# Weight conversion's low word moved to GpSimd, and a planner that changes its durations after the first batch

## The chip, the cores and the metric

The kernel runs on one core of one Trainium2 chip. The metric is the device time of one execution in microseconds (us); the median of several executions counts. TensorE is called PE, VectorE DVE, ScalarE ACT, GpSimd POOL, and SyncE, which issues most of the transfers here, SP.

## What is computed

```python
scores = scale * q @ k.T                       # 4 batches, 8 heads, 576 tokens, 64 wide
bias = -(cum[:, :, :, None] - cum[:, :, None, :])   # cum: running sum of max(s, 0)
scores = where(causal, -1e9, scores + minimum(bias, 0))
attn = softmax(scores) @ v                     # x: 2304 tokens x 512
h = x @ w_in                                   # 512 -> 2048
x = (h * (1 / (1 + exp(-1.702 * h)))) @ w_out  # 2048 -> 512
P = 8 rounds of row and column scaling of exp(x @ w_gate - max)   # 2304 x 8
out = sum over e of P[:, e] * (maximum(x @ w1[e], 0) @ w2[e])      # 8 experts
```

`w_in` and `w_out` come as 64-bit floats, all other inputs as 32-bit floats.

## The kernel before

The program has three stretches. In the first, attention is computed and its result goes through the first feed-forward layer (`w_in`, `w_out`), interleaved on PE. In the second, the last two token blocks go through that layer as one wide block. In the third, the eight experts run over three blocks of 768 tokens each; this is the longest one, and its products are built from seven half-size products each.

Attention goes batch by batch, and in a batch first over the first 256 query rows of the 8 heads, then over the other 320, so that there are 64 heads-and-halves, called heads in the code (`heads`, line 570 and on). A head has one or three units. A unit's scores are two matmuls into a PSUM bank (`sp<-one`, `sp<-two`; in the first eight heads one matmul `sp<-kf`); DVE adds the mask and takes the minimum (`sm<-sp,mask`), ACT takes the exponential (`ACTIVATE sm`), PE transposes (`turn`, tile `tp`), ACT and DVE split the result into two half-precision parts (`ph`, `pl`; in the first 14 heads a plain copy `pf`), and PE multiplies with the values (`op`). In the third unit of a later head, POOL clears 64 columns of `sm` before the transposes (`MEMSET sm`). A head's queries and keys are loaded (`kq`), rounded by ACT or DVE (`one`), their remainder taken by DVE, and one half copied by a transfer (`two<-one`).

The feed-forward layer takes 256 tokens and 256 hidden columns at a time: `mm1` (24 matmuls in two halves into `hp`), a tanh on ACT, a product on DVE, a split into `gh` and `gl`, and `mm2` (24 matmuls into `acc`). Its weights must first be converted. There are 32 chunks of 128 x 512 numbers (`conv`, line 525). A chunk is loaded as pairs of 32-bit words into `st`; ACT rebases the exponent of the high words (`Prelu`), ACT turns the top byte of each low word into three bits (`Copy` with a scale and an offset, line 536), DVE joins the two (`t<-st`), and `split` makes the rounded part (`wih`, `woh`, by ACT or DVE) and the remainder (`wil`, `wol`, by DVE).

The order on every engine is made by a planner at build time (`Sequencer`). Each call is recorded with a duration from `cost` and the calls that it depends on; `issue` keeps a clock for each engine; `settled` says when a tile will be ready, and adds 200 ns. The main loop (line 2033 and on) asks at the planner's present PE time which of six things can go next, in a fixed order: scale of the values, transposes of finished tokens, values, turn, scores, and only then a piece of the feed-forward layer. So that layer's matmuls fill PE where the planner believes attention isn't ready. Work of the other engines is held with a rank and issued as its engine comes free; conversion and the early preparation of the experts' weights have rank 2, the last. Until the layer's first piece, PE gets filler matmuls (`unread<-mask`) where its recent use is under half. `any_copy` gives a copy to DVE or ACT, whichever has less queued in the planner's clocks. From `begin_second` on (line 1888) `seq.fine` is set and other durations hold.

## Time and profile before

| | |
|---|---|
| median of 3 executions | 2006.13 us (2004.4 to 2006.52) |
| the profiled execution | 2004.02 us, of which the span from first to last instruction is 2002.3 us |
| busy in the span | PE 98%, weight loads 79%, DVE 74%, ACT 62%, POOL 4% |
| mean granted PE clock | 0.994 of full speed |
| HBM traffic | 157 GB/s over the span |

The profiled execution is the fastest of those shown; it lies 2.1 us under the median. A matmul's busy time overlaps that of its neighbours, so a busy PE is a PE that has work, not one at its peak. Times within the span count from its first instruction.

### The profile page before, as it was taken

What the parts mean: (1) busy time and instruction counts of PE and PEld (TensorE: products, weight loads), DVE (VectorE), ACT (ScalarE), POOL (GpSimd) and SP (SyncE); (2) the same over time, 40 slices, a digit from 0 to 9 for tenths busy, and PEclk for the clock granted to TensorE, in tenths of its full rate; (3) what the DMA queues carried; (4) which work ended last, traced back from release to release, by engine and by line L of the source; (5) the groups of instructions that cost most, each with busy time, mean ns of one, the idle gap of its engine ahead of it and who ended that gap; (6) DMA issues with size and microseconds to landing.
All of it is one profiled execution on the core that took longest, in us unless ns stands there. A gap on an engine that the chain in (4) does not pass through costs nothing.

```text
span 2002.3 us, 41146 instructions
## 1 busy us (share of the span) xinstructions
PE 1964.1 (98%) x15805; PEld 1578.6 (79%) x15805; DVE 1471.9 (74%) x3421; ACT 1249.3 (62%) x2576; POOL 87.2 (4%) x144
## 2 busy tenths in 40 slices
PE   7989999999999999999999999999999999999999
PEld 6888999999998677777777777777777777777777
DVE  7787888887853676988877766776786876777656
ACT  6787667675634575666666666656666666665333
POOL 1000000000000000000000111111101001111000
PEclk9999999999999999999999999999999999999999
DMA  8455455444226454475475566667557556566331
GB/s 253 126 187 176 123 141 155 130 130 118 76 69 213 156 198 151 159 257 182 156 256 145 131 184 176 181 171 203 161 130 244 152 156 181 163 172 182 119 129 43
DMA packets 230100, 322.12 MB, mean 161 GB/s; under 512 B 38272, under 2 KB 156224, under 8 KB 229904
## 3 DMA queue, kind: packets, MB, share of 16 engines
q1 hardware_dynamic: 216944, 295.90, 45.1%
q0 software_dynamic: 12960, 23.60, 8.2%
q8 instruction: 124, 2.03, 0.4%
q14 instruction: 72, 0.59, 0.1%
HBM read 230.85 MB, written 84.34 MB: 157 GB/s over the span
## 4 chain that ended last, share of the span: by engine, by line
PE 73%; DVE 10%; ACT 6%; DMA 2%; issue 1%; SPq 0%; ACTq 0%; DVEq 0%
PE C L307 16%; PE A L307 16%; PE D L307 16%; PE B L307 8%; PE hp L307 6%; PE acc L307 3%; ACT h L307 2%; PE accw L307 2%; DVE h L307 2%; PE op L307 1%; PE sp L307 1%; PE tp L307 1%; DVE hst L307 1%; DVE sa L307 1%; DMA kq<-in_qk_dram 1%
## 5 line engine op out<-in xcount | busy, mean ns | idle before, releaser
L307 PEld LDWEIGHTS <-h 128*128 128x128 f16 x6048 | 591.4, 98 | 85.4 <-issue 6.7
L307 PEld LDWEIGHTS <-w1o 128*128 128x128 f16 x4036 | 394.6, 98 | 255.1 <-issue 4.4
L307 PE MATMUL C<-xt,w1o 128*128 128x384 f16 x1152 | 218.6, 326 | 1.4 <-DVE hst L307 1.4
L307 PE MATMUL D<-xt,w1o 128*128 128x384 f16 x1152 | 218.4, 326 | 0.0
L307 PE MATMUL D<-w2o,h 128*128 128x256 f16 x1728 | 217.7, 273 | 0.2 <-ACT y L307 0.2
L307 PE MATMUL A<-xt,w1o 128*128 128x384 f16 x1152 | 214.8, 326 | 0.1
L307 PE MATMUL A<-w2o,h 128*128 128x256 f16 x1728 | 212.2, 273 | 1.7 <-ACT B L307 1.4
L307 PE MATMUL C<-w2o,h 128*128 128x256 f16 x1728 | 208.4, 273 | 1.9 <-DVE y L307 1.7
L307 DVE SCALAR_TENSOR_TENSOR h<-hst,h 128x768 f16<-128x768 f32 (+1 forms) x192 | 139.1, 755 | 55.9 <-ACT h L307 55.9
L307 ACT COPY C<-B 128x384 f32<-128x384 f32 (+1 forms) x168 | 71.4, 425 | 154.7 <-PE B L307 93.7
L307 PE MATMUL hp<-xh,wih 128*128 128x256 f32 (+1 forms) x512 | 154.4, 302 | 0.8 <-ACT xh L307 0.5
L307 PE MATMUL hp<-xl,wih 128*128 128x256 f32 (+1 forms) x512 | 152.1, 297 | 0.6 <-DVE xl L307 0.6
L307 PE MATMUL hp<-xh,wil 128*128 128x256 f32 (+1 forms) x512 | 151.8, 297 | 0.0
L307 POOL DMA_DIRECT2D acc_d<-y x90 | 77.8, 864 | 1224.4 <-DVE y L307 660.3
L307 ACT ACTIVATE h<-hst 128x768 f16<-128x768 f32 (+1 forms) x192 | 126.2, 678 | 3.8 <-DVE hst L307 3.7
L307 ACT ACTIVATE sm<-sm,stats 64x576 f32<-64x576 f32 (+4 forms) x160 | 93.7, 602 | 41.2 <-DVE stats L307 40.1
L307 PE MATMUL acc<-gh,woh 128*128 128x256 f32 x384 | 112.4, 293 | 0.0
L307 PE MATMUL B<-w2o,h 128*128 128x256 f16 x864 | 110.5, 273 | 0.1
L307 PE MATMUL acc<-gl,woh 128*128 128x256 f32 x384 | 109.9, 286 | 0.0
L307 PE MATMUL acc<-gh,wol 128*128 128x256 f32 x384 | 109.6, 285 | 0.0
L307 PE MATMUL B<-xt,w1o 128*128 128x384 f16 x576 | 109.3, 326 | 0.0
L307 ACT COPY B<-A 128x384 f32<-128x384 f32 (+1 forms) x168 | 70.3, 426 | 59.0 <-PE A L307 58.4
(238 smaller groups left out, 3877.0 us busy)
## 6 DMA issues: line engine op xcount, KB each, us to landing
xt<-xc_d SPq DMA_DIRECT2D x168, 384.0 KB
wm<-in_moe_w_dram SPq DMA_DIRECT2D x112, 256.0 KB
w2o<-w_d SPq DMA_DIRECT2D x56, 512.0 KB
wr<-in_moe_w_dram SPq DMA_DIRECT2D x112, 256.0 KB
w_d<-wo SPq DMA_DIRECT2D x98, 256.0 KB
acc_d<-y POOLq DMA_DIRECT2D x90, 256.0 KB, 4.9
kq<-in_qk_dram SPq DMA_DIRECT2D x32, 448.0 KB
st<-in_moe_w_in_dram SPq DMA_DIRECT2D x16, 512.0 KB
```

Source lines behind the costliest of these rows:

```text
L307: self.seq.submit(self.name, what, lambda: method(*args, **named), outs, ins, "accum_op" in named)
```

## The change

The diff has two halves. In `conv` the three bits of the low word come from one `tensor_scalar` on POOL in place of the `Copy` on ACT. In the planner, `rough` is set once 16 heads have their values prepared, which is the first batch. From then until `begin_second`, `cost` gives one plain duration per kind of work (no charge for a matmul's start, for a weight load, for a scalar operand), a call's end has no `tail`, and a dependency on the same engine counts like one on another. Before that point, the durations of 32-bit matmuls with few columns and of ACT instructions on strided or byte inputs are raised. "Low parts" in the change's name are the remainders that `any_less` takes; they are on DVE in both kernels.

```diff
--- before.py
+++ after.py
@@ -79,6 +79,7 @@
         self.rank = 0
         self.holding = False
         self.fine = False
+        self.rough = False
         self.slack = 0
         self.cold, self.since, self.streamed = True, 0.0, 0.0
         self.late = 0.0
@@ -135,9 +136,25 @@
             n *= x
         return n
 
+    @staticmethod
+    def strided(ap):
+        return abs(list(ap.ap)[-1][0]) > 1
+
     def cost(self, engine, what, out, ins, sums=False):
         n = max(self.size(x) for x in [out] + ins[:2])
         psum = any(x.space == PSUM for x in ins)
+        if self.rough and not self.fine:
+            if engine == "PE":
+                n = self.size(out)
+                if what == "transpose":
+                    return 2 * n / 2.4
+                slow = ins[0].dtype == F32 or ins[0].dtype == F32R and n < 256
+                return n * (4 if slow else 1) / 2.4
+            if engine == "DVE":
+                quick = what in ("tensor_copy", "tensor_scalar") and not psum
+                return 70 + n / (1.92 if quick else 0.96)
+            if engine == "ACT":
+                return 90 + n / 1.2 + 190 * sums
         if self.fine:
             if engine == "PE":
                 return self.size(out) * (4 if ins[0].dtype == F32 else 1) / 2.4 + (13 if ins[0].dtype == F32R else 2.7)
@@ -145,13 +162,17 @@
             n = self.size(out)
             if what == "transpose":
                 return 2 * n / 2.4 + 3
-            slow = ins[0].dtype == F32 or ins[0].dtype == F32R and n < 256
+            if ins[0].dtype == F32:
+                return 4 * max(n, self.size(ins[0])) / 2.4 + 10
+            slow = ins[0].dtype == F32R and n < 256
             return n * (4 if slow else 1) / 2.4 + (13 if ins[0].dtype == F32R else 2.7)
         by = any(self.size(x) == 1 for x in ins[1:]) and n > 1
         if engine == "DVE":
             quick = what in ("tensor_copy", "tensor_scalar") and not psum
             return 66 + 60 * by + n / (1.92 if quick else 0.96)
         if engine == "ACT":
+            if what == "activation" and (ins[0].dtype == U8 or self.strided(ins[0])):
+                n += 54
             return (50 if psum else 90) + 100 * by + 93 * sums + n / 1.2
         return 80 + n * {"memset": 0.3, "tensor_scalar": 2.7}.get(what, 2.24)
 
@@ -171,9 +192,11 @@
             op.stream = 0.36 if what == "matmul" and ins[0].dtype == F32 else 1.0
             sums = len(outs) > 1
             if engine == "PE":
-                op.load = 110 if BYTES[ins[0].dtype] == 4 else 27
+                op.load = 0 if self.rough else 110 if BYTES[ins[0].dtype] == 4 else 27
             op.cost = self.cost(engine, what, outs[0], ins, sums)
-            op.tail = {"DVE": 85, "ACT": 110}.get(engine, 0) + 90 * sums
+            op.tail = 0
+            if self.fine or not self.rough:
+                op.tail = {"DVE": 85, "ACT": 110}.get(engine, 0) + 90 * sums
         for ap, writes in [(x, False) for x in ins] + [(x, True) for x in outs]:
             name = ap.tensor.name
             if name in self.outside:
@@ -200,7 +223,7 @@
         if on.end is None:
             op.waits.add(on)
             on.after.append(op)
-        elif on.engine == op.engine != "PE" and not on.nbytes:
+        elif (self.fine or not self.rough) and on.engine == op.engine != "PE" and not on.nbytes:
             op.ready = max(op.ready, on.end + AFTER_OWN)
         elif on.engine != "PE" or op.engine != "PE":
             op.ready = max(op.ready, on.end + LATENCY.get((on.engine, op.engine), LATENCY.get(on.engine, 0)))
@@ -533,7 +556,7 @@
             t = (stage[0] if c < 4 * NP1 else mpool).tile([128, a, n], I32, tag="t", name="t64", bufs=2)
 
             nc.scalar.activation(out=f32(hw), in_=f32(hw), func=ACTF.Prelu, scale=F64_REBASE, alpha=F64_NEGATIVE)
-            nc.scalar.activation(out=lw, in_=top, func=ACTF.Copy, scale=2.0**-5, bias=-0.484375)
+            nc.gpsimd.tensor_scalar(out=lw, in0=top, scalar1=2.0**-5, scalar2=-0.484375, op0=ALU.mult, op1=ALU.add)
             nc.vector.scalar_tensor_tensor(
                 out=t, in0=hw, scalar=3, in1=lw, op0=ALU.logical_shift_left, op1=ALU.bitwise_or
             )
@@ -2039,7 +2062,9 @@
         more_scales()
         seq.run()
         now = seq.free["PE"]
-        for seq.slack in (SLACK, 0):
+        if not seq.rough and n_pv >= 2 * H:
+            seq.rough = True
+        for seq.slack in (0,) if seq.rough else (SLACK, 0):
             times = [can_vpow(), can_flush(), can_value(), can_turn(), can_score(), moe1_can()]
             which = next((k for k, x in enumerate(times) if x <= now), None)
         if at_first and seq.share() < SHARE:
```

**POOL, from its start-up on.** Rows carry the tiles' numbers: `st` is a chunk of weights, `sm` a unit's scores. Before:

```order
L307 MEMSET vf4_138 128x6
L307 MEMSET sm_676 64x64
L307 MEMSET sm_771 64x64
L307 MEMSET sm_882 64x64
L307 MEMSET sm_1009 64x64
```

The change:

```order
L330 TENSOR_SCALAR st_277<-st_277 128x512
L330 MEMSET sm_641 64x64
L330 TENSOR_SCALAR st_283<-st_283 128x512
L330 MEMSET sm_755 64x64
L330 TENSOR_SCALAR st_362<-st_362 128x512
L330 TENSOR_SCALAR st_416<-st_416 128x512
L330 TENSOR_SCALAR st_448<-st_448 128x512
L330 TENSOR_SCALAR st_500<-st_500 128x512
L330 MEMSET sm_853 64x64
```

The 32 new instructions stand between and ahead of the memsets, in one queue; eight stand ahead of the first memset, and 30 ahead of the ninth.

**PE, where the first batch ends.** `tp 128x64 x5` is the turn of its last unit. Before:

```order
L307 LDWEIGHTS pl
L307 MATMUL op<-v_131,pl 128x65
L307 MATMUL tp<-ident,sm 128x64 x5
L307 LDWEIGHTS ph
L307 MATMUL op<-v_131,ph 128x65
```

The change:

```order
L330 MATMUL hp<-xh,wih_84 128x256
L330 MATMUL hp<-xl,wih_84 128x256
L330 MATMUL hp<-xh,wil_85 128x256
L330 MATMUL tp<-ident,sm 128x64 x5
L330 MATMUL tp<-ident,sm 128x128 x3
L330 MATMUL sp<-one_114 128x256
L330 MATMUL sp<-two_115 128x256
```

Twelve `acc` and twelve `hp` matmuls, of which three are shown, now stand directly ahead of that turn, where there were values alone: before, this turn stands between the values of the two units ahead of it.

**PE, in the second half of the second batch.** Before, at the turn `tp 128x64 x5` of its first three-unit head:

```order
L307 LDWEIGHTS ph
L307 MATMUL op<-v_132,ph 128x64
L307 LDWEIGHTS pl
L307 MATMUL op<-v_130,pl 128x65
L307 MATMUL tp<-ident,sm 128x64 x5
L307 MATMUL sp<-one_114 128x512
L307 MATMUL sp<-two_115 128x512
L307 MATMUL hp<-xh,wih_2284 128x256
```

The change, at the next head:

```order
L330 MATMUL op<-v_130,pl 64x65
L330 MATMUL tp<-ident,sm 128x128 x3
L330 MATMUL sp<-one_114 64x288
L330 MATMUL sp<-two_115 64x288
L330 LDWEIGHTS ph
L330 MATMUL op<-v_131,ph 128x65
```

Here a turn is followed by two score matmuls and then by its own values, with no feed-forward matmul between; such a run of attention alone stands in both orders, one head later in the change.

## Rows read from the trace of the kernel before

**Rows 1.** Busy time by stretch: us, PE, weight loads, DVE, ACT, POOL, clock, DMA, GB/s.

```profile
0.00:41.00 41.00, 29.93 (x239) 23.66 (x240) 27.14 (x98) 24.54 (x49) 4.94 (x23) 0.96 0.86 255
41.00:105.00 64.00, 59.64 (x499) 52.75 (x500) 52.63 (x163) 51.05 (x92) 1.01 (x7) 0.95 0.45 139
105.00:175.00 70.00, 62.81 (x537) 58.86 (x537) 60.83 (x165) 58.02 (x118) 0.29 (x2) 0.91 0.62 194
175.00:574.00 399.00, 392.81 (x3845) 375.92 (x3844) 318.44 (x962) 261.35 (x541) 3.18 (x22) 1.00 0.44 126
574.00:800.00 226.00, 224.01 (x1541) 172.10 (x1540) 133.81 (x305) 118.89 (x251) 0.00 (x0) 1.00 0.48 164
800.00:2002.00 1202.00, 1194.86 (x9156) 895.28 (x9154) 879.07 (x1733) 735.50 (x1528) 77.80 (x90) 1.00 0.57 168
```

**Rows 2.** Waits of PE, 0 to 41 us: total us, times, longest.

```profile
PE sp L307 <- DMA kf<-aux: 3.4, 2, 1.7
PE unread L307 <- POOL mask L307: 2.4, 1, 2.4
PE sp L307 <- DVE stats L307: 1.7, 2, 1.5
```

**Rows 3.** Waits of PE, 41 to 105 us.

```profile
PE op L307 <- ACT gh L307: 0.9, 1, 0.9
PE op L307 <- ACT t L307: 0.3, 1, 0.3
PE op L307 <- ACT woh L307: 0.3, 1, 0.3
```

**Rows 4.** Timeline of PE where batch one ends: start, us, instruction, [idle before].

```profile
101.55 0.22 PE L307 MATMUL op<-v,ph 128*128 128x65 f16 x2 [0.93 <-DVE xg L307]
...
103.30 0.20 PE L307 MATMUL op<-v,pl 128*128 128x65 f16 x1 [0.69 <-DVE pl L307]
```

**Rows 5.** Waits of PE, 105 to 175 us.

```profile
PE sp L307 <- DMA two<-one: 2.9, 1, 2.9
PE tp L307 <- ACT sm L307: 1.2, 2, 0.9
PE sp L307 <- DVE stats L307: 0.8, 1, 0.8
PE hp L307 <- DVE xl L307: 0.6, 1, 0.6
PE hp L307 <- ACT xh L307: 0.5, 1, 0.5
```

**Rows 6.** Busy time by stretch, where the clock fell.

```profile
80.00:100.00 20.00, 19.27 (x153) 15.93 (x152) 15.68 (x57) 13.24 (x25) 0.43 (x3) 0.83 0.22 69
130.00:150.00 20.00, 17.14 (x136) 16.80 (x134) 15.42 (x43) 15.31 (x35) 0.00 (x0) 0.83 0.57 174
160.00:180.00 20.00, 17.42 (x139) 14.78 (x138) 15.50 (x39) 14.76 (x28) 0.15 (x1) 0.83 0.61 198
```

**Rows 7.** ACT's groups by shape, 0 to 200 us: busy us, mean ns.

```profile
L307 ACT ACTIVATE st<-st 128x512 int32<-128x512 uint8 x32 | 21.4, 675 | 0.0
L307 ACT ACTIVATE st<-st 128x512 f32<-128x512 f32 x32 | 21.3, 678 | 5.2 <-DMA st<-in_moe_w_out_dram 4.9 <-DMA st<-in_moe_w_in_dram 0.2
L307 ACT ACTIVATE sm<-sm,stats 128x512 f32<-128x512 f32 x11 | 7.9, 719 | 3.3 <-DVE stats L307 3.2
L307 ACT CAST woh<-t 128x512 fp32r<-128x512 f32 x12 | 7.4, 613 | 0.2 <-DVE t L307 0.2
```

**Rows 8.** DVE's groups by shape, 0 to 200 us.

```profile
L307 DVE CUSTOM_DVE_ANT_0 sm<-sp,mask 128x512 f32<-128x512 f32 x11 | 7.5, 685 | 1.0 <-PE sp L307 0.9
L307 DVE CAST woh<-t 128x512 fp32r<-128x512 f32 x4 | 1.7, 416 | 0.0
```

**Rows 9.** POOL's groups by shape, 0 to 600 us.

```profile
L307 POOL MEMSET mask<- 128x512 bf16 x1 | 0.5, 523 | 0.0
L437 POOL TENSOR_SCALAR_AFFINE_SELECT mask<-mask 128x128 bf16<-128x128 bf16 x1 | 0.3, 292 | 0.1
L307 POOL MEMSET v<- 128x5 f16 x2 | 0.1, 110 | 0.0
```

**Rows 10.** Chain that ended last, in order of time, one step of it.

```profile
476.14 2.88 PE acc L307 x24
```

**Rows 11.** Waits of PE, 175 to 574 us.

```profile
PE op L307 <- DVE stats L307: 1.9, 6, 0.7
PE op L307 <- DVE xg L307: 1.3, 1, 1.3
PE sp L307 <- DMA two<-one: 1.2, 2, 1.0
PE op L307 <- DVE pl L307: 0.8, 2, 0.7
```

## The prediction

> **What bounds the kernel now.** I read the stretches first [rows 1]. From 800 us on PE is busy 1194.9 of 1202 us, and from 574 to 800 us 224 of 226: nothing of the change reaches there except what is pushed into it. From 175 to 574 us PE lacks 6.2 us in 399. What can still be won lies ahead of 175 us, where PE is idle 11.1, 4.4 and 7.2 us and runs at 0.96, 0.95 and 0.91 of its clock. There DVE and ACT are nearly as busy as PE: from 105 to 175 us DVE 60.8, ACT 58.0 and PE 62.8 of 70 us. No engine is the bound by itself; PE waits at single places where a chain over DVE and ACT ends late, and the waits tell at which. Of the first 11.1 us, 2.4 us are the wait for the first mask and 3.4 us the wait for the first rows of keys [rows 2]; the change doesn't touch the transfers ahead of these. After clusters of idle time the granted clock is lower: 0.83 from 80 to 100, from 130 to 150 and from 160 to 180 us [rows 6]. A mean of 0.83 between 2.4 and 1.2 GHz is a third of 20 us at the low level, and so some 3.4 us of matmul work lost each time; before the second of these falls PE had waited 2.9 us for one transfer, before the third 1.2 and 0.8 us [rows 5].
>
> **The conversion.** Removed from ACT: 32 instructions of 675 ns, 21.6 us by the count, 21.4 us busy [rows 7], all within the first 175 us. Added on POOL: 32 instructions of 512 elements, with no row of their kind. The nearest below is the 523 ns memset of 512 elements, above four times the 292 ns of the only arithmetic there, on 128 elements, 1.17 us. I take 110 ns, the smallest memset, as the fixed part and scale the rest of the 292 ns: 0.11 + 4 x 0.182 = 0.84 us [rows 9], 27 us in all, between 17 and 37. POOL has 6 us of work there, so this is off every path unless it disturbs another engine. By the Trainium skill's "GPSIMD Engine Reference", section "Performance pitfalls for Q7 kernels", a read whose step is at most 8 bytes, as here, takes about 1.9 cycles an element; at the 1.2 GHz of its section "Specifications" an estimate is 0.81 us plus dispatch, and the sum would be the same.
>
> A chunk's chain also gets shorter: before, 678 and 675 ns stood in a row on ACT; now 0.84 us on POOL run beside 678 ns on ACT, which makes 0.5 us less before DVE joins them. Nobody on PE waits for a chunk by name, so I count this as nothing; were it longer, the cover is the feed-forward work of earlier chunks. POOL takes its queue in order, so a memset of `sm` can now stand behind a chunk that hasn't landed. ACT already waits for late chunks, 4.9 us in all [rows 7], with the exponentials that those memsets follow queued behind them. So this wait is no new one, and I count nothing. The weights' loads on SP keep their number; one load of values moves behind two loads of keys, and the scale on PE that needs it moves back by 3 us of matmuls. These go together at nothing.
>
> **Copies that change engine.** By the orders' counts ACT gets 13 copies more and DVE 13 fewer: 4 of each weight half, keys and small ones to ACT, 4 of `gh` to DVE. At 613 ns on ACT and 416 ns on DVE [rows 7, 8] that is about 8.0 us onto ACT and 5.4 us off DVE. So ACT sheds about 13.6 us net, and DVE about 5.4 us, of the 134 and 141 us that they are busy ahead of 175 us [rows 1].
>
> **What PE gets of it.** An engine that does less is worth only the waits that it ends late. Four terms:
> - To 41 us: PE's longest wait but the start-up is 1.5 of 1.7 us on a score bank that DVE hasn't read [rows 2]. In the new order the transposes of finished tokens stand between those scores, 8 matmuls. I take 1.5 us off, between 0 and 1.7. Four filler matmuls fewer are nothing.
> - 41 to 105 us: values wait 0.9, 0.3 and 0.3 us for ACT work queued ahead of their copy [rows 3]. ACT has a tenth less to do; I take half, 0.7 us, between 0 and 1.5.
> - Where batch one ends, PE waits 0.93 and 0.69 us among values and turns [rows 4]. The new order puts 24 feed-forward matmuls ahead of the turn; 24 of them last 2.88 us [rows 10], more than both waits. I take 1.6 us off, between 0 and 1.6.
> - 105 to 175 us: the 2.9 us wait is for a transfer [rows 5] that shares the queues with weight loads; the new order also puts three weight loads ahead of such a transfer, so I leave it. The waits of 1.2 and 0.8 us come from a run of attention without feed-forward work; it stands in the new order too, one head later. The 0.6 and 0.5 us behind finished tokens lie on DVE and ACT; of them I take 0.7 us off, between 0 and 1.1.
>
> That is 4.5 us. I count no change of the clock: one cluster goes, but the two that the clock paid for remain. Between the ends, it could give or take 3.4 us for each of three falls.
>
> **The rough durations.** They hold from the preparation of the last values of batch one to the wide block. The planner then believes every engine to be a little faster, PE most (it loses the 13 ns on each matmul of 107). What is left there is 6.2 us of waits, of which 5.2 us are these four [rows 11]. A turn needs 0.685 us on DVE and 0.719 us on ACT after its scores [rows 7, 8], plus handovers, some 2 us. Counting matmuls, I find five turns of the new order from 105 us on with under 1.7 us of matmuls between scores and transposes, two in the old one: about +1 us. Work of rank 2 moves later, and DVE has some 15 us less of it ahead of a given turn in batches three and four: about -1 us, from the waits on DVE. It moves into the wide block, where DVE has 92 of 226 us free [rows 1]. Together nothing, between -3 and +4 us. The other edit, one slack instead of two, does nothing: the old loop never stops at its first pass, since the `break` stands behind a `continue`, so slack 0 always decided.
>
> **Sum.** The profiled execution took 2004.0 us, 2.1 us under the median, so its terms are taken off the median, which a new measurement is likelier to meet: 2006.1 - 4.5 = **2001.6 us**.
>
> **Rivals.**
> *The gain is given back.* PE is busy 93% from 41 to 105 us already; a wait that goes can show up as the next one, for the same chains, half a turn later, and the transfer's wait and the clock's falls are left. For it: clusters of attention alone stand in both orders. Against it: the first and third terms are replaced by real matmuls. Time: 2005.5 us.
> *POOL holds up DVE.* If DVE can't read while POOL does, 27 us of POOL fall on an engine that is busy 113.5 of 134 us from 41 to 175 us [rows 1]. Were each DVE instruction in the way held for half of a POOL instruction, DVE would get 13.5 us and lose 5.4: 121.6 of 134, 91%. It decides as soon as DVE's own queue, not PE, ends the waits, at about nine tenths; then the 8.1 us reach PE, plus one more fall of the clock, 3.4 us, and none of my 4.5 us is won: 2006.1 + 8.1 = 2014 at most, 2011 if two thirds arrive. For it: the joins, remainders and products are two-input instructions on DVE. Against it: no row shows the two engines at work together, except memsets. The Trainium skill, "GPSIMD Engine Reference", section "Specifications", says that POOL shares its SBUF interfaces with VectorE and contends with DVE instructions that have two SBUF inputs or use a two-port mode; by that rule this rival would be the likeliest. No run here shows it yet, and the trace can neither agree nor disagree.
> *Turns come too early.* 96 units follow the switch. If each came 85 to 110 ns early, by the dropped ends of DVE and ACT, PE would wait some 9 us more: 2011 us with my gain off. It decides if most turns stand at the shortest distance; by the count five do.
>
> **How the numbers follow.** About 0.2%, 4 us, is what a measurement here tells from no change. My forecast gets 0.45; most of it lies beyond 4 us, its own range is 1994 to 2002. The gain given back gets 0.35, within 0.2%. POOL against DVE gets 0.13 and turns too early 0.07, both slower: 0.20. The low end takes half of the idle time ahead of 175 us that isn't start-up, 8 of 16.8 us, and two falls of the clock, 6.8 us: 1991. The high end takes in most of both slower rivals: 2012.
>
> **What would show it.** Right: ACT's byte instructions gone and its busy time to 175 us down by some 13 us; POOL's new instructions at 0.6 to 1.2 us; the waits of rows 4 gone; PE idle ahead of 175 us at 18 us instead of 22.6. Wrong: DVE's means for the same shapes (685 ns, 416 ns) longer where POOL runs; new waits of turns on ACT behind 175 us; a wait of a turn on a POOL memset; or a clock below 0.95 where it was 1.00.

## The result, and the profile after

The changed kernel takes **1988.69 us**, the median of four executions (1982.78 to 1989.66); the kernel before took 2006.33 us beside it, again of four. The ratio is 0.991, with a 95% interval of 0.9889 to 0.993: faster by 18 us, between 14 and 22. The forecast was 2001.6 us with a range of 1991 to 2012. The sign was right; the time lies 2.3 us under the low end, and the gain is four times the 4.5 us that I had counted. The profiled execution took 1988.55 us, 1986.7 us of it the span.

The stretches of the changed kernel answer to [rows 1], with the same columns (us, PE, weight loads, DVE, ACT, POOL, clock, DMA, GB/s):

```profile
0.00:41.00 41.00, 35.46 (x203) 29.18 (x203) 24.23 (x81) 19.48 (x39) 9.91 (x29) 0.71 0.75 222
41.00:105.00 64.00, 59.80 (x535) 53.04 (x536) 59.74 (x178) 52.98 (x96) 11.27 (x22) 1.00 0.58 186
105.00:175.00 70.00, 67.99 (x645) 64.55 (x644) 64.20 (x169) 54.74 (x112) 9.89 (x13) 1.00 0.58 174
175.00:574.00 399.00, 395.78 (x3810) 376.24 (x3809) 311.93 (x946) 258.49 (x528) 3.21 (x22) 1.00 0.42 121
574.00:800.00 226.00, 224.05 (x1572) 169.88 (x1571) 150.54 (x344) 134.11 (x286) 0.00 (x0) 1.00 0.52 174
```

Ahead of 175 us PE is idle 5.5, 4.2 and 2.0 us, 11.7 in all instead of 22.6, and from there to 574 us 3.2 instead of 6.2. The largest step is from 105 to 175 us: 645 matmuls stand there instead of 537, where up to 105 us both kernels had done 738. The wide block starts at 566.3 instead of 582.6 us, 16.3 us sooner, so all of the gain is won ahead of it. DVE got 16.7 us more to do in the wide block (150.5 against 133.8), and PE doesn't feel it.

The clock, in the three stretches of [rows 6] and ahead of them:

```profile
10.00:30.00 20.00, 19.85 (x96) 17.51 (x95) 13.56 (x52) 11.27 (x25) 4.42 (x9) 0.50 0.94 285
80.00:100.00 20.00, 19.82 (x189) 18.00 (x189) 17.38 (x60) 14.16 (x28) 1.84 (x5) 1.00 0.44 140
130.00:150.00 20.00, 19.43 (x178) 18.68 (x177) 19.09 (x49) 16.69 (x36) 5.93 (x7) 1.00 0.59 184
160.00:180.00 20.00, 18.82 (x180) 16.79 (x179) 16.11 (x36) 15.44 (x28) 1.85 (x3) 1.00 0.70 216
```

All three falls are gone, and in this execution one at the start has come: 0.50, the 1.2 GHz level, from 10 to 30 us. The 10 us ahead of it look alike in both kernels (PE busy 6.1 us, and 6.0 before), so these rows don't say why. Over the whole span the clock gives this execution nothing: its mean is 0.994 in both profiles. Worked out from the rows, the low clock cost 1.6, 3.2 and 6.3 us of matmul work in the three stretches to 175 us before, 11.1 in all, and 11.9 us (0.29 x 41) in the first stretch of the change.

The waits of PE from 41 to 105, from 105 to 175 and from 175 to 574 us answer to [rows 3, 5, 11] (total us, times, longest):

```profile
PE vbp L330 <- DVE xl L330: 1.2, 1, 1.2
PE xtp L330 <- DVE xg L330: 0.8, 1, 0.8
PE op L330 <- DVE stats L330: 0.6, 1, 0.6
...
PE op L330 <- DVE pl L330: 0.5, 2, 0.4
PE sp L330 <- DMA two<-one: 0.5, 1, 0.5
...
PE op L330 <- DVE stats L330: 1.6, 6, 0.3
PE op L330 <- DVE xg L330: 0.6, 2, 0.4
```

The transfer that cost 2.9 us in [rows 5] costs 0.5, the waits of `tp` on ACT and of `sp` on DVE are gone, and so are the 0.93 and 0.69 us of [rows 4].

POOL's new row, and the DVE groups that joined the low words, of the changed kernel (0 to 600 and 0 to 200 us: busy us, mean ns):

```profile
L330 POOL TENSOR_SCALAR st<-st 128x512 int32<-128x512 uint8 x32 | 24.7, 771 | 100.3 <-DMA st<-in_moe_w_out_dram 43.1 <-DMA st<-in_moe_w_in_dram 35.7 <-DVE pl L330 12.1
...
L330 DVE SCALAR_TENSOR_TENSOR t<-st 128x512 int32<-128x512 int32 x32 | 23.0, 724 | 0.2
L330 DVE TENSOR_TENSOR wol<-t,woh 128x512 fp32r<-128x512 f32 x16 | 12.1, 768 | 0.1
L330 DVE CUSTOM_DVE_ANT_0 sm<-sp,mask 128x512 f32<-128x512 f32 x12 | 8.2, 681 | 0.7 <-PE sp L330 0.7
```

and of the kernel before:

```profile
L307 DVE SCALAR_TENSOR_TENSOR t<-st 128x512 int32<-128x512 int32 x32 | 21.7, 683 | 3.1 <-ACT st L307 2.5 <-DVE gl L307 0.5
L307 DVE TENSOR_TENSOR wol<-t,woh 128x512 fp32r<-128x512 f32 x16 | 10.9, 680 | 0.0
```

POOL took 771 ns, where I had 0.84 us. DVE's two-input instructions grew: `t<-st` by 41 ns, `wol` by 88; the mask's minimum, one input of which lies in PSUM, did not (685 to 681). planner_alone, described below, is the changed kernel without the POOL instructions, and has the old durations:

```profile
L330 DVE SCALAR_TENSOR_TENSOR t<-st 128x512 int32<-128x512 int32 x32 | 21.7, 682 | 0.1
L330 DVE TENSOR_TENSOR wol<-t,woh 128x512 fp32r<-128x512 f32 x16 | 10.9, 684 | 0.8 <-ACT woh L330 0.8
```

So the growth comes with POOL. Its size hangs on the order too: pool_alone, with the same 32 POOL instructions, has 697 and 684 ns.

### The profile page after: what moved, and what is told of

Its sections match the earlier page's. It is cut to its first block, busy times and chain, and to the rows that moved or that the text cites. A ratio compares the mean times of both kernels' runs of the same rounds, so it can differ in the third digit from the quotient of the medians.

```text
span 1986.7 us, 41192 instructions
## 1 busy us (share of the span) xinstructions
PE 1962.2 (99%) x15801; PEld 1577.1 (79%) x15801; DVE 1474.0 (74%) x3408; ACT 1240.2 (62%) x2557; POOL 112.3 (6%) x176
## 3 DMA queue, kind: packets, MB, share of 16 engines
q1 hardware_dynamic: 216944, 295.90, 45.6%
## 4 chain that ended last, share of the span: by engine, by line
PE 82%; DVE 8%; ACT 6%; DMA 3%; issue 1%; SPq 0%; ACTq 0%; DVEq 0%
PE C L330 17%; PE A L330 16%; PE D L330 16%; PE hp L330 8%; PE B L330 8%; PE acc L330 5%; PE sp L330 3%; PE op L330 3%; PE tp L330 2%; ACT h L330 2%; PE accw L330 2%; DVE h L330 2%; DMA kq<-in_qk_dram 1%; PE accx L330 1%; DVE hst L330 1%
## 5 line engine op out<-in xcount | busy, mean ns | idle before, releaser
L330 DVE SCALAR_TENSOR_TENSOR h<-hst,h 128x768 f16<-128x768 f32 (+1 forms) x192 | 138.9, 753 | 55.9 <-ACT h L330 55.9
```

Source lines behind the costliest of these rows:

```text
L330: self.seq.submit(self.name, what, lambda: method(*args, **named), outs, ins, "accum_op" in named)
```

## The experiments

Each kernel was timed beside the kernel before on the same chip; the median of the kernel before there was 2006.3 us beside the change and 2003.6 to 2004.7 us beside the others, so the ratios are what compares. The last columns are from one profile of each: PE's idle time and mean granted clock from 105 to 175 us, and idle time from 245 to 565 us. The profiles of corrections_alone and best_0 are of their slowest executions (1999.9 and 2001.2 us).

| kernel | median us | ratio, 95% interval | idle, clock 105-175 | idle 245-565 |
|---|---|---|---|---|
| before | 2003.6 to 2006.3 | 1 | 7.2, 0.91 | 6.1 |
| the change | 1988.7 | 0.991 (0.9889 to 0.993) | 2.0, 1.00 | 2.1 |
| pool_alone | 1996.5 | 0.9968 (0.9957 to 0.9979) | 4.1, 0.95 | 6.2 |
| planner_alone | 1988.3 | 0.9924 (0.9912 to 0.9936) | 2.5, 0.95 | 2.1 |
| no_switch | 1996.8 | 0.9961 (0.9948 to 0.9974) | 4.2, 0.98 | 6.8 |
| switch_alone | 1994.2 | 0.995 (0.9938 to 0.9962) | 2.2, 0.96 | 2.1 |
| corrections_alone | 1996.0 | 0.9957 (0.9945 to 0.9969) | 4.0, 0.95 | 6.4 |
| before_margin | 1998.7 | 0.9971 (0.996 to 0.9982) | 6.5, 0.95 | 7.7 |
| rough_vector | 2002.7 | 0.9994 (0.9985 to 1.0003) | 4.0, 0.98 | 8.5 |
| rough_pe_cost | 1988.9 | 0.9921 (0.9908 to 0.9933) | 3.7, 0.98 | 3.0 |
| early_4 | 2004.7 | 1.0001 (0.9991 to 1.0011) | 5.9, 0.91 | 6.2 |
| pe_dearer | 2022.0 | 1.0083 (1.0069 to 1.0097) | 7.5, 1.00 | 19.8 |
| pe_cheaper | 1986.9 | 0.9909 (0.9896 to 0.9923) | 1.1, 1.00 | 1.7 |
| vector_dearer25 | 1992.4 | 0.9936 (0.9923 to 0.9948) | 2.3, 0.98 | 3.1 |
| vector_dearer40 | 1991.8 | 0.9937 (0.9923 to 0.9951) | 2.1, 1.00 | 2.4 |
| latency120 | 1999.9 | 0.9978 (0.9966 to 0.9991) | 5.3, 0.95 | 5.0 |
| pe_late4 | 1996.8 | 0.9965 (0.9951 to 0.9978) | 6.5, 0.93 | 2.0 |
| pe_corr | 1984.2 | 0.9896 (0.9882 to 0.9909) | 3.2, 1.00 | 1.9 |
| best_c2 | 1983.2 | 0.9894 (0.9878 to 0.991) | 4.1, 0.98 | 1.4 |
| best_0 | 1992.6 | 0.9943 (0.9924 to 0.9962) | 5.0, 0.95 | 3.7 |

### Which half of the change

Three theories stood at first. A: ACT's relief wins. B: the planner's durations win. C: the order before was an unlucky one, and any other gains several us, so that parts don't add up.

**pool_alone**: the kernel before with the POOL line alone.

```diff
-            nc.scalar.activation(out=lw, in_=top, func=ACTF.Copy, scale=2.0**-5, bias=-0.484375)
+            nc.gpsimd.tensor_scalar(out=lw, in0=top, scalar1=2.0**-5, scalar2=-0.484375, op0=ALU.mult, op1=ALU.add)
```

> The kernel before, with only the low word's three bits moved to POOL; the planner's durations as before. Theory A (ACT's relief ends the waits of PE ahead of 175 us, and with the waits the falls of the clock there): 1993 to 1999 us, PE idle from 41 to 175 us at 8 us or less instead of 11.6, mean clock there 0.97 or more. Theory B (the planner's other durations place the feed-forward work better): 2003 to 2008 us, clock from 105 to 175 us near 0.91 as before. Theory C (any change reorders the work, and the clock's falls are a matter of where a run of attention alone happens to stand): anything from 1990 to 2012 us, and no sum of parts holds.

**planner_alone**: the changed kernel with that line back on ACT (the diff above, turned round).

> The changed kernel with the low word's bits back on ACT; all of the planner's edits stay. Theory A: 2000 to 2006 us, since ACT is as busy as before. Theory B: 1988 to 1994 us. Theory C: anything from 1985 to 2012 us.

**no_switch**: the changed kernel without the setting of `rough`, so POOL's line and the corrected durations.

```diff
-        if not seq.rough and n_pv >= 2 * H:
-            seq.rough = True
```

> The changed kernel, but the planner never goes over to rough durations; POOL's part and the corrected durations of small 32-bit matmuls and of ACT on strided or byte inputs stay. Theory A: 1988 to 1994 us, as the changed kernel. Theory B, if the switch is what counts: 1996 to 2006 us, with waits of PE from 175 to 574 us back at 6 us instead of 3.2. Theory C: anything.

**switch_alone**: the kernel before with `rough` and all that it selects, but without the corrected durations and without POOL. Against the changed kernel, beside the POOL line:

```diff
-            if ins[0].dtype == F32:
-                return 4 * max(n, self.size(ins[0])) / 2.4 + 10
-            slow = ins[0].dtype == F32R and n < 256
+            slow = ins[0].dtype == F32 or ins[0].dtype == F32R and n < 256
...
-            if what == "activation" and (ins[0].dtype == U8 or self.strided(ins[0])):
-                n += 54
```

> The kernel before, with only the switch to rough durations; bits on ACT and no corrected durations. Up to the switch, at about 90 us, the order is that of the kernel before, with the same waits and clock. Theory A: 2003 to 2008 us. Theory B, if the switch is what counts: 1992 to 1999 us, all of it won behind 90 us. Theory C: anything.

In us of a median of 2004, POOL alone gives 6.4, the planner's half 15.2, POOL with the corrections 7.8, the switch alone 10.0 and the whole change 18.0. The planner's half gives nearly all without POOL, and its interval overlaps that of the whole. The four parts share one mark: idle time from 245 to 565 us falls to 2.1 us where the switch is in, and stays at 6 to 7 where it isn't. So B holds behind 245 us. The 6 to 8 us of the kernels without the switch remained.

**corrections_alone**: the kernel before with the corrected durations only.

```diff
-            slow = ins[0].dtype == F32 or ins[0].dtype == F32R and n < 256
+            if ins[0].dtype == F32:
+                return 4 * max(n, self.size(ins[0])) / 2.4 + 10
+            slow = ins[0].dtype == F32R and n < 256
...
+            if what == "activation" and (ins[0].dtype == U8 or self.strided(ins[0])):
+                n += 54
```

> Before plus the corrected durations alone (the float32 matmul's, and 54 elements more for an ACT copy from bytes or strided words); bits on ACT, no switch. If the switch alone carries the planner's gain and adds to the rest: as before, within 3 us (2001 to 2006 against 2003.6). If the corrections bring their own share (planner's edits together 15.3 us less, the switch alone 9.4): 5 to 7 us less, about 1997.5, gained ahead of 105 us, since the words that they correct stand only there. If any new order wins several us (order luck): 4 to 9 us less, with the gain spread over the stretches and 175 to 574 us among them.

**before_margin**: a constant of the planner that the change doesn't touch.

```diff
-                t = max(t, x[3].end + 200 + self.slack)
+                t = max(t, x[3].end + 220 + self.slack)
```

> Before with one constant moved that has nothing to do with the change: the time that the planner adds to a turn's due time for its scores to settle, 220 instead of 200 ns. If the change's gain comes of what its parts say: within 3 us of before (2001 to 2006). If before's order is an unlucky one, so that any other wins several us: 1994 to 1999.

The corrections give 8.6 us, and the unrelated constant gives 5.8. POOL with the corrections gave 7.8, no more than the corrections alone. So C holds for some 6 us ahead of 245 us: POOL's 6.4 us are what an unrelated nudge of the order brings too, and no run shows that ACT's relief is worth anything by itself. It is no law that any order wins: rough_vector and early_4, below, gain nothing.

### Which durations

**rough_vector** and **rough_pe_cost** are switch_alone with one side of `rough` each. The first keeps DVE's and ACT's rough durations, the dropped tails and the dropped gap behind an engine's own result, and takes out PE's:

```diff
-            if engine == "PE":
-                n = self.size(out)
...
-                op.load = 0 if self.rough else 110 if BYTES[ins[0].dtype] == 4 else 27
+                op.load = 110 if BYTES[ins[0].dtype] == 4 else 27
```

The second keeps PE's rough durations alone; against switch_alone:

```diff
-            if engine == "DVE":
-                quick = what in ("tensor_copy", "tensor_scalar") and not psum
-                return 70 + n / (1.92 if quick else 0.96)
-            if engine == "ACT":
-                return 90 + n / 1.2 + 190 * sums
...
-                op.load = 0 if self.rough else 110 if BYTES[ins[0].dtype] == 4 else 27
+                op.load = 110 if BYTES[ins[0].dtype] == 4 else 27
...
-            if self.fine or not self.rough:
+            if True:
...
-        elif (self.fine or not self.rough) and on.engine == op.engine != "PE" and not on.nbytes:
+        elif on.engine == op.engine != "PE" and not on.nbytes:
```

> Before plus the switch, with only VectorE's and ScalarE's durations, tails and the gap behind an engine's own result made rough; PE's durations and weight loads stay as they were. If the vector side carries the switch's gain (a turn is placed sooner, and less early preparation is queued ahead of it on VectorE): 1994 to 1996, with PE idle of 175 to 574 us at 2 to 4 us instead of 5 to 6. If PE's shorter durations carry it: 2001 to 2005. If any new order wins: 1994 to 1999 for this and for the margin run alike.

> Before plus the switch, with only PE's durations made rough (2.7 and 13 ns less for a matmul, 3 for a transpose); all else as before. If PE's shorter durations carry the switch's gain (the planner sees less time pass on PE, so gives less early work to the others in it): 1994 to 1996. If the vector side does: 2001 to 2005. If any new order wins: 1994 to 1999.

This pair names the side that wins: PE's durations alone give 15.8 us, as much as the planner's whole half and more than twice what the unrelated constant gave; the vector side alone gives nothing that the interval tells from none, and its idle time from 245 to 565 us rises. Planned matmuls that are 2.7 or 13 ns too short are enough. The two sides don't add up, though: both together (switch_alone) give 10.0 us, less than PE's alone, and yet leave less idle time from 245 to 565 us, 2.1 against 3.0.

### Why shorter planned matmuls win

Theory D was that the planner, which sees less time pass on PE, hands out less early preparation for the experts ahead of each turn. The trace shows that this moves. The last step on the experts' early inputs, in the kernel before, in rough_pe_cost and in early_4 (min, median, max ns; first to last start us):

```profile
L307 DVE TENSOR_TENSOR xb<-xa,xb x56: 343/352/360, 421.4 to 579.1; 128x192 f16<-128x192 f32 x56
```

```profile
L320 DVE TENSOR_TENSOR xb<-xa,xb x56: 324/351/359, 466.6 to 609.4; 128x192 f16<-128x192 f32 x56
```

```profile
L307 DVE TENSOR_TENSOR xb<-xa,xb x56: 339/351/360, 494.4 to 626.0; 128x192 f16<-128x192 f32 x56
```

**early_4** is the kernel before with that preparation held back by a condition and no duration changed. (`4 * H` is 32 heads, which ends the second batch; where the expectations of this kernel and of pe_late4 say "fifth batch's first head", read the third batch's.)

```diff
-        if n_conv < len(chunks):
+        if n_conv < len(chunks) or n_pv < 4 * H:
```

> Before with all durations as they were, but the preparation for the second expert layer's weights and inputs (rank 2) asked for only from the value preparation of the fifth batch's first head on, instead of as soon as the conversion is over. Theory D (the switch's smaller PE durations win because the planner then gives less early preparation ahead of each turn): TensorE idle of 175 to 574 us falls from 6.2 to 3 to 4.5 us, the last early input step starts after 600 us instead of at 579, and the time is 1994 to 1999. Theory C (any new order wins): 1994 to 1999 too, but with the idle time of that stretch left at 6 to 9 us. If durations themselves matter: 2001 to 2006.

**pe_dearer** and **pe_cheaper** give rough_pe_cost other doses:

```diff
-                return n * (4 if slow else 1) / 2.4
+                return n * (4 if slow else 1) / 2.4 + (26 if ins[0].dtype == F32R else 5.4)
```

```diff
-                return n * (4 if slow else 1) / 2.4
+                return n * (4 if slow else 1) / 2.4 - 4
```

> Before plus the switch, with PE's durations after it made longer instead of shorter (5.4 and 26 ns a matmul on top of its columns instead of 2.7 and 13). Theory D: the planner gives more early preparation ahead of the turns, the last early input step comes ahead of 570 us, idle of 175 to 574 us rises to 8 to 14 us, and the time is 2004 to 2012. Theory C (any new order wins): 1994 to 1999.

> Before plus the switch, with PE's durations after it shorter still (4 ns a matmul less than its columns). Theory D: idle of 175 to 574 us stays at 2 to 4 us, time 1986 to 1991 as with the rough PE durations alone, since little idle time is left there to win; further down only if turns ahead of 175 us gain too. Theory C: 1994 to 1999.

early_4 holds the preparation back further than rough_pe_cost does, and neither its time nor its idle time moves. By itself this isn't the end of D, since what early_4 empties is the stretch from 175 to 245 us; from 245 to 565 us its DVE and ACT are as busy as before. But no_switch has less work on them there and more idle time, and pe_late4, below, has nearly as much as before and a third of the idle time. From 245 to 565 us (columns as above), of early_4 and no_switch:

```profile
245.00:565.00 320.00, 313.75 (x3087) 299.65 (x3087) 258.27 (x792) 215.31 (x445) 2.60 (x18) 1.00 0.46 132
```

```profile
245.00:565.00 320.00, 313.22 (x3037) 300.45 (x3035) 254.32 (x775) 206.41 (x439) 2.31 (x16) 0.99 0.44 124
```

So D falls: how much early work there is doesn't by itself decide the waits. The dose, though, answers in order. In the same stretch, of pe_dearer, the kernel before, rough_pe_cost and pe_cheaper:

```profile
245.00:565.00 320.00, 300.18 (x2906) 281.60 (x2904) 244.80 (x752) 198.72 (x415) 2.46 (x17) 0.99 0.40 114
```

```profile
245.00:565.00 320.00, 313.86 (x3095) 300.85 (x3093) 260.01 (x797) 212.39 (x446) 2.60 (x18) 1.00 0.44 124
```

```profile
245.00:565.00 320.00, 317.03 (x3101) 304.23 (x3100) 256.88 (x773) 204.83 (x430) 2.31 (x16) 1.00 0.43 121
```

```profile
245.00:565.00 320.00, 318.29 (x3101) 304.30 (x3101) 254.78 (x775) 204.23 (x429) 2.31 (x16) 1.00 0.42 121
```

PE lacks 19.8, 6.1, 3.0 and 1.7 us, in the order of the planned durations. pe_dearer waits there for the operands of [rows 11], longer in all, and for others besides (`hp` for `t`, `tp` for `sm`):

```profile
PE op L320 <- DVE stats L320: 4.2, 5, 2.0
PE op L320 <- DVE xg L320: 3.9, 4, 1.1
PE hp L320 <- DVE t L320: 2.3, 2, 1.4
PE tp L320 <- ACT sm L320: 1.8, 4, 0.6
PE sp L320 <- DMA two<-one: 1.7, 3, 0.8
```

Theory E then: the plan is a race between engines. Where the planned PE runs quicker than the real one, or the planned DVE and ACT slower, the planner finds a result late in terms of matmuls, puts more matmuls ahead of its reader, and the real result is there in time. F: it is something of PE's own durations, such as which matmuls come first.

**vector_dearer25** and **vector_dearer40** leave PE's planned durations alone; after the same point every DVE and ACT operation is planned 25 or 40 ns longer.

```diff
-            return 66 + 60 * by + n / (1.92 if quick else 0.96)
+            return 66 + 25 * (self.rough and not self.fine) + 60 * by + n / (1.92 if quick else 0.96)
...
-            return (50 if psum else 90) + 100 * by + 93 * sums + n / 1.2
+            return 25 * (self.rough and not self.fine) + (50 if psum else 90) + 100 * by + 93 * sums + n / 1.2
```

**latency120** adds a fixed 120 ns to each planned hand-over to PE instead.

```diff
-            op.ready = max(op.ready, on.end + LATENCY.get((on.engine, op.engine), LATENCY.get(on.engine, 0)))
+            op.ready = max(op.ready, on.end + LATENCY.get((on.engine, op.engine), LATENCY.get(on.engine, 0)) + 120 * (op.engine == "PE" and self.rough and not self.fine))
```

**pe_late4** is rough_pe_cost with the switch at `4 * H`, so that the order up to some 240 us is that of the kernel before.

```diff
-        if not seq.rough and n_pv >= 2 * H:
+        if not seq.rough and n_pv >= 4 * H:
```

> Before plus the switch, PE's durations as they were, but every VectorE and ScalarE operation planned 25 ns longer after it. Theory E (what wins is the planned ratio: where the plan's TensorE is quick, or its VectorE and ScalarE slow, a vector result stands further behind the matmuls that cover it, and the real one is there in time): as the rough PE durations, idle of 175 to 574 us 3 to 5 us instead of 6.2, 1988 to 1996. Theory F (it is something of PE's own durations, such as which matmuls the planner puts first): 2001 to 2006. Theory C (any new order): 1994 to 1999 with that idle at 6 to 9 us.

> Before plus the switch, VectorE's and ScalarE's operations planned 40 ns longer (25 ns gave 1992.4). Theory E: idle of 245 to 565 us 2 to 3 us (6.1 before, 3.2 with 25 ns), idle of 105 to 175 us 2 to 4 us, 1986 to 1993. If the 25 ns won by a lucky order: 1994 to 2004.

> Before plus 120 ns on each hand-over to TensorE that the planner counts after the switch; no duration changes. If theory E holds by a fixed reserve for each result: idle of 175 to 574 us 3 to 5 us, 1990 to 1997. If it needs the ratio (less other work queued on VectorE and ScalarE for each matmul, so that a delay does not build up over a batch): 1998 to 2005, idle still 5 to 8 us. Theory C: 1994 to 1999.

> Before plus PE's rough durations only from the value preparation of the fifth batch's first head on, so that the order up to about 240 us is before's own. Theory E in that part alone: up to 240 us as before (first feed-forward matmuls near 42 us, clock about 0.91 over 105 to 175 us, idle about 7 us there), TensorE idle of 245 to 565 us about 3 us instead of 6.1, and 1999 to 2002 in all; most of the 15 us then belongs to the order between 90 and 240 us. If the end of the attention carries more than that: under 1998. Theory C gives no such split.

From 245 to 565 us, of vector_dearer25, vector_dearer40, rough_vector, latency120 and pe_late4 (its 105 to 175 us ahead):

```profile
245.00:565.00 320.00, 316.85 (x3112) 303.44 (x3111) 258.69 (x780) 209.60 (x434) 2.46 (x17) 1.00 0.42 121
```

```profile
245.00:565.00 320.00, 317.65 (x3123) 303.97 (x3122) 255.94 (x774) 208.74 (x434) 2.45 (x17) 1.00 0.42 120
```

```profile
245.00:565.00 320.00, 311.52 (x3038) 294.34 (x3037) 258.06 (x785) 209.39 (x441) 2.46 (x17) 1.00 0.43 120
```

```profile
245.00:565.00 320.00, 314.96 (x3083) 300.34 (x3082) 261.82 (x799) 212.17 (x445) 2.46 (x17) 1.00 0.44 125
```

```profile
105.00:175.00 70.00, 63.55 (x556) 60.00 (x553) 61.72 (x168) 59.05 (x121) 0.29 (x2) 0.93 0.64 203
...
245.00:565.00 320.00, 317.99 (x3141) 305.12 (x3142) 258.44 (x784) 210.34 (x440) 2.47 (x17) 1.00 0.42 121
```

F falls: with PE's durations untouched, dearer vector work brings 12.7 us and takes that stretch from 6.1 to 3.1 and 2.4 us of idle time; cheaper vector work (rough_vector) had taken it to 8.5. The expectation for 175 to 574 us was met only behind 245; vector_dearer25 is idle 2.8 us from 175 to 245 us, where the kernel before is idle 0.0. A fixed 120 ns leaves 5.0 us idle there and gives 4.4 us of time, less than before_margin's nudge. That speaks for the ratio and against a reserve for each hand-over, but only one such reserve was tried, and why it does less isn't settled.

That more matmuls stand ahead of the reader can be counted in the orders, though I did so with the times known. The reader that waits most in this stretch is the values' matmul (`op`). Of the 64 units of batches three and four, I counted those with less than 2.3 us of matmuls, at the plain durations of `rough`, between the end of their transposes and their first values. There are 30 in the kernel before, 33 in pe_dearer and in rough_vector, 32 in latency120, and 30 in early_4 and in before_margin; 24 in rough_pe_cost and in pe_cheaper, 26 and 24 in vector_dearer25 and vector_dearer40, 22 in pe_late4 and 25 in the change. In all twenty kernels those with 5.0 us of idle time or more have 30 to 37, those with less 21 to 29. The limit of 2.3 us was picked for this, and the same count between scores and transposes doesn't part the kernels.

pe_late4 splits the gain. Its first 240 us are as before, to the low clock of 0.93, and it wins 7.0 us, more than the 2 to 5 that I expected (and little more than before_margin's 5.8, but here idle time from 245 to 565 us falls, by 4.1 us, where there it rose); the rest of the 15.8 us lies between 90 and 240 us. There order luck and reserve can't be parted cleanly: idle time from 105 to 175 us is 1.1 to 3.7 us in the kernels with PE's rough durations from 90 us on and bits on ACT or POOL, but 4.1 in best_c2.

### A faster order

**pe_corr** joins the two parts that won most: rough_pe_cost with the corrected durations (the diff of corrections_alone), bits on ACT. **best_c2** takes 2 ns more off each planned matmul, **best_0** is pe_corr with the switch at the start. Their diffs against pe_corr:

```diff
-                return n * (4 if slow else 1) / 2.4
+                return n * (4 if slow else 1) / 2.4 - 2
```

```diff
-        if not seq.rough and n_pv >= 2 * H:
-            seq.rough = True
+        seq.rough = True
```

> Before plus the switch with PE's durations alone made rough, plus the corrected durations; bits on ScalarE. Theory D with each part's gain in its own stretch (corrections ahead of 105 us, PE's durations behind it): 1983 to 1988, the fastest so far. Theory C: 1988 to 1997, no gain over the rough PE durations alone (1988.9).

> The fastest so far with PE's durations 2 ns a matmul shorter still behind the switch. Theory E with little left to win (idle of 175 to 574 us was 2.4 us): 1982 to 1986, no difference that can be told. If the reserve is already too large, so that turns come late and the wide block fills with early work: 1987 to 1995.

> The fastest so far (corrected durations plus the switch with PE's durations alone made rough, 1984.2), with the switch made at the start instead of at about 50 us. Theory E with the same reserve in the first batch: idle ahead of 105 us falls by 1 to 4 us, 1980 to 1984. Against it: ahead of 50 us TensorE waits on transfers and half clock, which no reserve shortens: 1984 to 1988.

pe_corr and best_c2 are the fastest here, 20.8 and 21.2 us under the kernel before. Their intervals overlap that of the change, so they aren't shown to be faster than it, but they do without POOL and without rough vector durations. best_0 loses 9.4 us of that gain, against its expectation: with the switch ahead of the first batch the order behind that is another one too (3.7 us of idle time from 245 to 565 us instead of 1.9), so how much of the loss is the first batch's isn't shown.

## Why the prediction was wrong

**The rough durations: "Together nothing, between -3 and +4 us."** This is the step that failed. They give 10.0 us alone, and PE's part of them alone 15.8. I had read the code rightly (the planner "believes every engine to be a little faster, PE most") and stopped at the vector side: dropped tails bring turns early (+1), less early work lies ahead of them (-1). Both were the wrong places. The first exists: rough_vector has 2.4 us more idle time from 245 to 565 us. But the five short turns that I counted cost nothing in the change: among its waits of `tp` from 105 to 574 us there is none on ACT or DVE. The second isn't what wins, by early_4, no_switch and pe_late4. What I left out is that PE's shorter durations push the other way, and harder: idle time from 245 to 565 us fell from 6.1 to 3.0 us by them alone, and to 2.1 in the change. I also looked for the gain only in the four waits of [rows 11]; half of it lies between the switch and 240 us, and there I had no term for the luck of the order, for which an unrelated constant stands with 5.8 us.

**"I count no change of the clock."** Right over the span, by luck, and wrong in its reason. I took it that "the two that the clock paid for remain", for two clusters that the new order kept; but all three falls of [rows 6] are gone. From 105 to 175 us the clock's 0.91 became 1.00, some 6.3 us of matmul work (0.09 x 70), beside 5.2 us less idle time; the transfer's wait, which I left as it was, fell from 2.9 to 0.5 us. A new low stretch at the start took as much back, so that both profiles have a mean of 0.994. What the profiled execution gained ahead of the wide block, 16.3 us, is for the most part idle time: some 14 us less of it to 574 us. Nor does idle time as a sum tell the clock: from 105 to 175 us pe_dearer has 7.5 us of it at 1.00, planner_alone 2.5 at 0.95.

**The conversion.** Prices right: POOL 771 ns for a forecast of 840 and bounds of 523 and 1170. ACT's busy time to 175 us fell from 133.6 to 127.2 us, half of the 13.6 counted, but with 109 more matmuls done by then. Against planner_alone, whose work to that point is alike (138.9 us), the move takes off 11.7.

**The four PE terms, -4.5 us.** PE's idle time ahead of 175 us is 11.7, where 18 was forecast. The end of batch one came as said. By stretch the terms fit badly: 5.5, 0.2 and 5.2 us went where 1.5, 2.3 and 0.7 were counted. The largest wait from 41 to 105 us, 1.5 us of `sp` on DVE, stands neither in [rows 3] nor in the sum; it is gone in the change. And these terms took ACT's relief as their reason, and corrections_alone and before_margin win more than 4.5 us without it. A direction that an unrelated 20 ns also gives isn't evidence for the reason. As far as these terms go, the right sign was luck.

**The slack loop does nothing**: with the old loop the order is the same on every engine.

**Rivals.** The gain given back: no. POOL against DVE: there, but small. The two-input groups grew by 41 ns x 32 and 88 ns x 16, 2.7 us, where the rival needed 13.5, and planner_alone without POOL has the old durations; no wait of PE from 41 us on names POOL. The Trainium skill, "GPSIMD Engine Reference", section "Specifications", says that POOL contends with DVE instructions of two SBUF inputs; the trace agrees in kind, since the minimum with one PSUM input didn't grow, and gives it a size. The rival's own sum was wrong too: its 2014 us "at most" leaves out the 3.4 us for a fall of the clock that it names, with which it would be 2017.6. Turns too early: the mechanism shows in rough_vector and, from the other side, in pe_dearer, 16.6 us slower.

## What to carry to other kernels

Where a planner sets the order as here, its durations need not be a forecast made exact; they can serve as a reserve to be set: plan the critical engine a little quick or the feeding engines a little slow, and look at the idle time of the critical engine for the sign. Before a reason is given for a gain of a few tenths of a per cent, nudge an unrelated constant of the planner and see what that brings; here it was 5.8 us. Read the granted clock by stretch and over the span: three falls went here, and the mean over the span stayed as it was.

## What the runs showed beyond that

The same order starts differently from one execution, or chip, to another. The orders of the kernel before, switch_alone, early_4 and pe_late4 are the same up to some 90 us, yet the mean granted clock to 41 us was 0.96, 0.88, 0.88 and 0.92 in their profiles, and the first feed-forward matmul came at 42.2, 45.6, 44.9 and 43.0 us. In the changed kernel's profile it came at 51.7 us after a stretch at 0.50, and the 9.5 us were made good by 105 us, with 738 matmuls done in both. The four executions of the changed kernel go with it: three at a mean clock of 0.994 took 1988.6 to 1989.7 us, the one at 0.998 took 1982.8. The falls in the middle, however, seem to belong to the order: the kernel before, early_4 and pe_late4, alike up to some 160 us and longer, show 0.91, 0.91 and 0.93 from 105 to 175 us, in one profile each.

The clock of whole executions doesn't make the gains. The kernel before ran 74 times beside the experiments, at mean clocks of 0.990 to 0.997; the five executions at 0.990 took 2009.6 to 2011.1 us, and a straight line through all 74 gives 1.1 us for each 0.001. Its mean is 0.994, and that of each other kernel 0.994 to 0.997: by that line 3.4 us at the most.
